# 44 zero matmuls of 128 rows in place of 60 of one row, ahead of the first transform of a Fourier and feed-forward kernel

## The chip, the cores and the metric

The kernel runs on one core of a Trainium2 chip. The metric is the device time of one execution in microseconds (us). The kernel before takes 2027.63 us (median of 7 runs, from 2026.54 to 2028.21).

## The reference

The input x holds 8 sequences of 3008 rows by 256 channels. The real part of its two-dimensional Fourier transform goes row by row through a feed-forward layer with the ELU function:

```python
X = np.fft.fft(np.fft.fft(x, axis=1), axis=2)
h = X.real.reshape(B * S, D) @ w_in            # (24064, 256) @ (256, 2048)
g = np.where(h > 0.0, h, np.exp(np.minimum(h, 0.0)) - 1.0)
return g @ w_out                               # (24064, 2048) @ (2048, 256)
```

The weights arrive as 64-bit floats; the kernel sees them as pairs of 32-bit words.

## The kernel before

**The steady part.** The symmetry of a real input lets the kernel do one column of the sequence transform for two output rows. Its 8 x 1504 columns are cut into tiles of 256. A tile takes eight steps, and each step treats two of the 16 blocks of 128 hidden units: TensorE multiplies the cosine half of the transform (ring buffer Rr) by folded weights Wc and the sine half (Ir) by Ws, VectorE, ScalarE and GpSimd form the ELU of the sum and of the difference, and TensorE multiplies the results by the second weights into four accumulators in PSUM (pA to pD).

**The order of work.** All work is put into one list of events with due times (`at`, line 983; a step's period is 4.8), sorted by time, and then emitted. Nearly every compute instruction is pinned, so each engine runs its own instructions in just that order. Events with times below zero are the preamble. This case is about the preamble.

**What the preamble does**, with the names that the profile shows:

- SyncE (SP) issues the loads: the first chunk of w_in (`raw`, line 193), two of the four quarters of x for sequence 0 (`xl`, lines 153 and 154; GpSimd issues the other two as indirect transfers, line 144), the channel matrix `CC` (line 964), the first cosine and sine matrices `MC` (`load_mats`, line 319: MC00, later MC10, and at last MC01 and MC11), and further chunks of the weights.
- A weight chunk is turned from 64-bit words into f32 by `fields` (VectorE, lines 211 and 217), `power` (ScalarE, line 359 by way of `act`), `round` (VectorE line 242, for some chunks GpSimd line 356) and `scale` (VectorE, lines 254 and 260).
- `fold_x` (line 413; instructions on lines 419 and 439) adds and subtracts the quarters of x into the inputs of the transforms: `e` for the cosine, `o` for the sine. `fold_first` (line 464) makes `xb`, the input for one extra channel.
- TensorE's order (every matmul is on line 347): the zero matmuls into bank M; `fold_chunk(0)`, eight matmuls `H<-w,CC` that fold weight chunk 0; `R_even`, six matmuls into pA and six into pB (`<-MC,e`); `x_even`, six into pC and six into pD (`<-MC,xb`); `I_even`, six into pA and six into M (`<-MC,o`); then the first step's matmuls, `fold_chunk(1)` and so on.
- ScalarE's order: `put_chunk(0)` (copies the folded chunk to Ws and Wc), `power` of w_in chunk 1, the copy of pA for `R_even` (`bs`), the copy of pC for `x_even`.
- VectorE's order: the folds of x, `fold_first`, `fields` and `round` of w_in chunk 1, `scale` of it, then `plus` and `minus` (line 353) of `R_even` into Rr, the same of `x_even` into Rb, then `fields` of w_in chunk 2, and so on. The first step's `even_part` (line 708, tile E) also needs `wex`, which SP brings in two hops: `wx<-Ws` (line 385) and `wex<-wx` (line 387). On SP that second hop stands behind `Ir<-Rb` (line 1036), which waits for `x_even`.

**The lines that change.** `zero` is made on line 333 and cleared on line 334. The loop on lines 959 and 960 is the first thing in TensorE's queue:

```python
mm(idle, zero[:, 0:128], zero[:, 0:1].to_broadcast([1, 512]), True)
```

Its weights are one row of 128 zeros, its moving operand is one zero that is read 512 times, and `idle` is PSUM bank M. Nothing reads what these matmuls write; bank M is written anew by `I_even`.

Of the kernel before, what the change touches and what calls it, by code (L numbers as in the profile page):

```python
# [10 lines left out]
BF = mybir.dt.bfloat16  # L11
# [66 lines left out]
def kernel(  # L78
# [17 lines left out]
    cpool = ctx.enter_context(tc.tile_pool(name="consts", bufs=1))  # L96
# [233 lines left out]
    pick = cpool.tile([128, 32], FP, tag="pick")  # L330
    nc.vector.memset(R4, 0.0)
    nc.vector.memset(Rx4, 0.0)
    zero = cpool.tile([1, 264], BF, tag="zero")
    nc.vector.memset(zero, 0.0)
    row_tables()
    r128_dr = dpool.tile([NB, HALF], FP, tag="r128", name="r128")
# [4 lines left out]
    def bank(tag):  # L341
        bufs = 3 if tag == "H" else 1
        return ppool.tile([128, 512], FP, tag=tag, bufs=bufs, name=tag)

    def mm(out_, lhsT, rhs, start, stop=True):
        pin(
            nc.tensor.matmul(  # L347
                out_, lhsT=lhsT, rhs=rhs, start=start, stop=stop, skip_group_check=True
            )
        )  # L350
# [377 lines left out]
    def exp_neg(ap):  # L728
        act(ap, ap, func=AF.Exp, scale=-1.0)
# [226 lines left out]

    state = {}
    idle = bank("M")
    for _ in range(60):
        mm(idle, zero[:, 0:128], zero[:, 0:1].to_broadcast([1, 512]), True)  # L960
    exp_neg(warm)
    w1_chunks[0].load()
    L_first = load_x(0)
# [291 lines left out]
```

## Time and profile before

| what | value |
|---|---|
| median of 7 runs | 2027.63 us |
| the profiled execution, its own time | 2033.98 us |
| its span, first to last instruction | 2031.9 us |
| TensorE busy | 1990.4 us (98%), 8878 matmuls |
| VectorE / ScalarE / GpSimd busy | 1290.1 / 858.4 / 1349.8 us |
| mean granted TensorE clock | 0.994 |
| DMA bytes | 71.60 MB, mean 35 GB/s |

Engines: PE is TensorE's matmul, PEld its weight load, DVE VectorE, ACT ScalarE, POOL GpSimd, SP SyncE; a q behind a name is the engine's queue, which also issues transfers. In `out<-in`, `128*128` is rows by columns of the weights and `128x256` the moving operand. A matmul's recorded duration holds the time through the array too, so the rate of a stream of matmuls is read from the distance between starts, or from the pieces of the chain of waits, which don't overlap. The chain of waits follows the work that ended last back to what released each piece. The clock column (PEclk) is 1.00 where the record shows no throttle.

### The profile page before, as it was taken

How to read it: one execution, taken by the hardware profiler on the slowest of the kernel's cores; microseconds unless marked ns; L12 is line 12 of the kernel's file. 1: busy time of each engine (PE TensorE's matmuls, PEld its weight loads, DVE VectorE, ACT ScalarE, POOL GpSimd, SP SyncE). 2: the span in 40 equal slices, each digit the busy share in tenths (PEclk: the TensorE clock that was granted, in tenths of full speed). 3: DMA queues.
4: the chain of work that ended last, by engine and by line, in shares of the span. 5: the costliest groups of instructions: out<-in, count | busy, mean ns of one | idle time of the engine just before them, and what ended most of it. 6: DMA issues, size and time to landing. Idle time of an engine off the chain costs nothing.

```text
span 2031.9 us, 26762 instructions
## 1 busy us (share of the span) xinstructions
PE 1990.4 (98%) x8878; PEld 1659.3 (82%) x8878; DVE 1290.1 (63%) x2353; ACT 858.4 (42%) x1646; POOL 1349.8 (66%) x1843
## 2 busy tenths in 40 slices
PE   8889899999999999999999999999999999999997
PEld 4678688888888888888888888888888888888886
DVE  6976456666566666666566665666656665566665
ACT  1444334444344443444344444444434444344443
POOL 1688666777477764877657775677757776455564
PEclk9999999999999999999999999999999999999999
DMA  7218410120001210121111111002110010100101
GB/s 304 81 28 8 93 20 11 29 76 16 11 14 27 73 20 14 17 50 42 25 16 19 42 43 28 11 19 73 19 21 11 19 22 14 16 11 13 19 11 21
DMA packets 256253, 71.60 MB, mean 35 GB/s; under 512 B 244512, under 2 KB 245302, under 8 KB 255604
## 3 DMA queue, kind: packets, MB, share of 16 engines
q1 hardware_dynamic: 253780, 57.32, 15.1%
q0 software_dynamic: 2336, 12.59, 1.9%
q8 instruction: 70, 1.15, 0.2%
q14 instruction: 67, 0.55, 0.1%
HBM read 45.02 MB, written 24.80 MB: 34 GB/s over the span
## 4 chain that ended last, share of the span: by engine, by line
PE 90%; DVE 3%; SPq 2%; DMA 2%; POOL 2%; issue 1%; ACT 0%; DVEq 0%; POOLq 0%; ACTq 0%
PE H L347 36%; PE pC L347 16%; PE pB L347 15%; PE pD L347 15%; PE pA L347 7%; POOL G L356 1%; PE M L347 1%; SPq L558 1%; DMA x<-in_x_dram 1%; DVE E L708 1%; SPq L893 0%; DVE G L734 0%; DVE pow L211 0%; DVE w L260 0%; DVE pow L254 0%
## 5 line engine op out<-in xcount | busy, mean ns | idle before, releaser
L356 POOL TENSOR_TENSOR G<-G 128x256 f32<-128x256 f32 x1504 | 1083.2, 731 | 607.1 <-DVE G L734 436.2
L708 DVE SCALAR_TENSOR_TENSOR E<-Rb,wex,H 128x256 f32<-128x256 f32 x752 | 328.0, 477 | 651.3 <-PE H L347 651.1
L359 ACT ACTIVATE G<-H 128x512 f32<-128x512 f32 x376 | 224.5, 597 | 975.9 <-DVE G L718 975.9
L347 PE MATMUL H<-Ir,Ws 128*128 128x256 f32 x1504 | 388.4, 381 | 10.4 <-DVE E L708 10.3
L347 PE MATMUL pC<-G,WT 128*128 128x256 f32 x1504 | 390.3, 382 | 2.3 <-DVE u L353 2.3
L347 PE MATMUL H<-Rr,Wc 128*128 128x256 f32 x1504 | 386.4, 379 | 0.0
L347 PEld LDWEIGHTS H<-Rr,Wc 128*128 128x128 f32 x1504 | 285.1, 190 | 53.2 <-issue 2.5
L347 PEld LDWEIGHTS H<-Ir,Ws 128*128 128x128 f32 x1504 | 279.8, 190 | 58.5 <-DVE E L708 13.2
L347 PEld LDWEIGHTS pC<-G,WT 128*128 128x128 f32 x1504 | 282.6, 190 | 54.2 <-issue 14.0
L718 DVE SCALAR_TENSOR_TENSOR G<-E,H 128x512 f32<-128x512 f32 x376 | 256.0, 681 | 26.5 <-POOL G L356 2.0
L734 DVE SCALAR_TENSOR_TENSOR G<-G,H 128x512 f32<-128x512 f32 x376 | 253.6, 675 | 27.8 <-ACT G L359 27.8
L734 DVE SCALAR_TENSOR_TENSOR G<-M,G 128x512 f32<-128x512 f32 x376 | 256.7, 683 | 0.0
L347 PE MATMUL pB<-G,WT 128*128 128x256 f32 x752 | 229.9, 387 | 5.4 <-POOL G L356 5.3
L359 ACT ACTIVATE G<-G 128x512 f32<-128x512 f32 x376 | 233.4, 621 | 0.0
L347 PE MATMUL pA<-G,w 128*128 128x256 f32 x752 | 224.5, 380 | 4.1 <-DVE Ir L353 4.0
L359 ACT ACTIVATE M<-G 128x512 f32<-128x512 f32 x376 | 224.4, 597 | 0.0
L347 PE MATMUL pB<-G,w 128*128 128x256 f32 x752 | 224.1, 380 | 0.0
L347 PE MATMUL pD<-G,WT 128*128 128x256 f32 x752 | 223.9, 379 | 0.0
L347 PE MATMUL pD<-G,w 128*128 128x256 f32 x752 | 223.7, 379 | 0.0
L359 ACT ACTIVATE M<-M 128x512 f32<-128x512 f32 x376 | 221.1, 588 | 0.1
L347 PEld LDWEIGHTS pB<-G,WT 128*128 128x128 f32 x752 | 138.5, 190 | 40.0 <-POOL G L356 23.3
L347 PEld LDWEIGHTS pA<-G,w 128*128 128x128 f32 x752 | 142.8, 190 | 24.4 <-issue 4.4
(131 smaller groups left out, 1363.8 us busy)
## 6 DMA issues: line engine op xcount, KB each, us to landing
out_dram<-ot SPq DMA_DIRECT2D x504, 32.0 KB
xl<-in_x_dram SPq DMA_DIRECT2D x16, 768.0 KB
MC<-dft_mats SPq DMA_DIRECT2D x4, 1131.0 KB
out_dram<-ot SPq DMA_DIRECT2D x256, 2.0 KB
Rb<-r SPq DMA_DIRECT2D x10, 376.0 KB
raw<-in_moe_w_in_dram SPq DMA_DIRECT2D x6, 512.0 KB
raw<-in_moe_w_out_dram SPq DMA_DIRECT2D x6, 512.0 KB
out_dram<-ot SPq DMA_DIRECT2D x64, 28.0 KB
```

The costliest lines, as they stand in the source:

```text
L347: nc.tensor.matmul(out_, lhsT=lhsT, rhs=rhs, start=start, stop=stop, skip_group_check=True)
L356: pin(nc.gpsimd.tensor_tensor(out=o, in0=a, in1=b, op=op))
L359: pin(nc.scalar.activation(out=o, in_=i, func=func, **kw))
L558: nc.sync.dma_start(out=t[:, s0:s1], in_=bass.AP(tensor=xt, offset=x.offset + row * ND + 128, ap=[[SEQ * ND, NB], [step * ND, s1 - s0], [1 ...
L708: nc.vector.scalar_tensor_tensor(out=S.E[:, c], in0=Rb[:, cols(i)], scalar=wex[:, f : f + 1], in1=S.H[:, c], op0=ALU.mult, op1=ALU.add,)
L718: nc.vector.scalar_tensor_tensor(out=two(S.G[:, 0:512])[:, :, ::-1], in0=two(S.E), scalar=2.0, in1=two(S.H), op0=ALU.mult, op1=ALU.subtract,)
L734: nc.vector.scalar_tensor_tensor(out=o, in0=e, scalar=-1.0, in1=h, op0=ALU.add, op1=ALU.max)
```

## The change

The tile of zeros becomes 128 rows by 128 columns. The loop issues 44 matmuls instead of 60, and each uses all 128 rows of the array; the moving operand is a zero column of 128 rows, read 512 times. Nothing else differs.

```diff
-    zero = cpool.tile([1, 264], BF, tag="zero")
+    zero = cpool.tile([128, 128], BF, tag="zero")
     nc.vector.memset(zero, 0.0)
...
     idle = bank("M")
-    for _ in range(60):
-        mm(idle, zero[:, 0:128], zero[:, 0:1].to_broadcast([1, 512]), True)
+    for _ in range(44):
+        mm(idle, zero, zero[:, 0:1].to_broadcast([128, 512]), True)
```

## The prediction

> **What bounds the kernel now.** The page first: PE is busy 98% of the span, and the chain of work that ended last is 90% PE. From 120 us on, all that PE waits for comes to 12.6 us (6.0 for POOL's xe, 3.7 and 2.3 and 0.6 for three others), so from there a PE-bound stream follows whose work the change leaves alone. What the change touches lies ahead of 120 us, so I read the chain of waits for the first 60 us; the columns are start, length, engine, tile, line.
>
> ```profile
> 1.20 25.78 PE M L347 x60
> 26.98 3.55 PE H L347 x8
> 30.52 1.90 PE pA L347 x6
> 32.43 1.90 PE pB L347 x6
> 34.33 1.91 PE pC L347 x6
> 36.23 1.92 PE pD L347 x6
> ...
> 38.25 1.00 DVE Rb L353 x2
> ```
>
> The 60 zero matmuls stand on the chain with all their 25.78 us. The first useful matmuls follow them without a gap, and VectorE's Rb at 38.25 waits for the last of these. So the zeros delay the start; how far they can shrink depends on what else is late.
>
> **The rate of a zero matmul.** The rows of the tile zero, then TensorE's timeline:
>
> ```profile
> L347 PE MATMUL M<-zero x60: 602/629/629, 1.2 to 26.3; 1*128 1x512 bf16 x60
> ```
>
> ```profile
> 26.91 3.62 PE L347 MATMUL H<-w,CC 128*128 128x256 f32 x8
> ...
> 56.35 1.89 PE L347 MATMUL H<-w,CC 128*128 128x256 f32 x8
> ```
>
> Zeros start (26.35 - 1.20)/59 = 0.426 us apart. The same eight matmuls H<-w,CC take 3.45 us from their first start to the next tile's at 26.91, and 1.73 at 56.35: 0.431 against 0.216 each. Right behind the zeros TensorE ran at half rate, and at 30.5 the transform pA runs at 0.317 for 377 columns, full rate. So 25 us of unbroken one-row matmuls did not open the clock, and 3.45 us of full-row matmuls did. The clock column reads 1.00 here; durations decide, since its first recorded change is the later one:
>
> ```profile
> 47.00:48.00 1.00, 0.00 (x0) 0.00 (x0) 1.00 (x4) 0.91 (x2) 0.00 (x0) 0.65 0.95 358
> 54.00:55.00 1.00, 1.00 (x4) 0.57 (x3) 0.90 (x2) 0.00 (x0) 0.00 (x0) 0.94 0.63 219
> ```
>
> In the clock column, the third from the end, a mean of 0.65 and of 0.94 puts the drop to half at 47.30 and the rise at 54.1. Finer stretches give drops at 71.2 and 91.7, rises at 74.6 and 95.1. The distances, 6.8, 17.1, 3.4, 17.1 and 3.4 us, are multiples of 3.4: the clock seems to be decided on a grid of 3.41 us. Full-row work from 49.15 needed 4.95 us to open it, from 71.63 2.95; a drop came after 2.6 to 3.6 us without a matmul.
>
> **The change, term by term.**
>
> *Removed:* 16 matmuls. At 0.426 that is 6.8 us on the chain.
>
> *Changed:* the other 44 use all rows. The trace has no full-row zeros. One bound is that they run like the one-row zeros: 44 x 0.426 = 18.8, ending near 20.1. The other is that they open the clock as H<-w,CC did. Half rate then lasts between 2.95 us and, if the start falls just behind a grid point, 6.8 (two windows). In D us at half rate D/0.426 matmuls run, and the rest take 0.213 each (0.426 x 0.216/0.431): 44 x 0.213 + D/2 = 10.9 to 12.8, ending at 12.1 to 14.0. I take this one: the nearest rows, full-row work on this engine, opened the clock each time, and what differs is only the values.
>
> The Trainium skill ("TensorE: Matmul & The Clock Gate", Part 1) says that some 3.4 us of sustained matmul activity open the gate, with no word of rows. The 25.78 us row speaks against that. By the rule alone the old zeros would have run fast from about 5 us on, and only 16 x 0.213 = 3.4 us would go.
>
> *The memset* of zero (0.17 us) becomes wider and shorter; R of 128x32 f32 took 0.09. At most 0.1 us, on the chain; taken as nothing.
>
> **What is late next.** With the zeros over by 14.0, fold_chunk(0) runs at full rate (1.73) until 13.9 to 15.8; its weight chunk left DVE by 8.9. Then the transforms need e, and DVE's timeline gives the rest:
>
> ```profile
> 16.20 1.95 DVE L419 TENSOR_TENSOR e<-e,e 128x768 f32<-128x768 f32 x2
> ...
> 24.65 0.69 DVE L242 SCALAR_TENSOR_TENSOR w<-raw,w 128x512 f32<-128x512 uint32 x1
> 31.86 0.69 DVE L254 SCALAR_TENSOR_TENSOR pow<-raw,pow 128x512 int32<-128x512 int32 x1 [6.51 <-ACT pow L359]
> 32.59 0.69 DVE L260 SCALAR_TENSOR_TENSOR w<-w,pow 128x512 f32<-128x512 f32 x1
> 34.44 0.55 DVE L353 TENSOR_TENSOR Rr<-bs,pB 128x377 f32<-128x377 f32 x1 [1.16 <-PE pB L347]
> ...
> 38.25 0.55 DVE L353 TENSOR_TENSOR Rb<-bs,pD 128x377 f32<-128x377 f32 x1 [2.74 <-PE pD L347]
> ```
>
> The reader is to see the brackets: idle time before an instruction and who ended it. DVE sat idle 6.51 + 1.16 + 2.74 = 10.4 us, each time because PE was late (the 6.51 through ACT, whose power of chunk 1 stands behind put_chunk, and that waited 16.2 us for PE H). Without PE's lateness DVE runs on: L242 ends at 25.34, L254 and L260 end by 26.8, R_even's plus, minus and one column take 1.07 (34.44 to 35.51), so Rb could start at 27.8.
>
> Does PE make that? e is ready at 18.15. pA to pD take 7.6 at full rate, ending at 25.8. But PE idles from 13.9-15.8 to 18.15, so the clock may close; half rate for up to 4.95 us (the row of 49.15) costs 2.5, and pD ends at 28.3. So Rb starts between 27.8 and 28.4 instead of 38.25: **9.9 to 10.4 us earlier**. I take 10.3, as DVE's own queue hides most of a closed clock. Here the same page of the Trainium skill speaks against the change: it warns that a PE gap over about 3 us returns the gate to half rate. The row of 47.3 agrees; the rule would charge the transforms some 1.7 us (half of 3.4), nearly all under DVE.
>
> *Matrices:* MC00 was issued at 2.70. SP's waits tell when loads landed:
>
> ```profile
> SPq L193 <- DMA raw<-in_moe_w_in_dram: 0.2, 1, 0.2
> ```
>
> ```profile
> SPq L319 <- DMA MC<-dft_mats: 0.8, 1, 0.8
> ```
>
> The first ended at 16.9: a w_in chunk issued behind MC00 had landed. The second ended at 22.3, for MC10, which I_even needs only after 25.8. Both match loads landing in the order of issue.
>
> *wex:* the one transfer that loses its cover. DMA is full until 35.0 (share 0.93 to 1.0, then 0.09). wx<-Ws would be issued near 23.5 instead of 30.97, and wex<-wx near 30.3 at the earliest. It took 3.9 us (40.64 to 44.55). If wx is not held up, wex lands by 34.2; if both wait for the queue to drain, at 35 + 1.1 (wx's own wait at 52.67) + 3.9 = 40.0. The first E, at 48.31 now, is due at 38.0. So 0 to 2.0 us; I take 0.3, as a 1 KB read behind one 512 KB load should be quicker than with three behind it.
>
> *Behind Rb* the chain goes DVE, ACT, POOL, DVE on chunk 2, whose data landed by 19; it moves as a whole. Chunk loads of line 193 at 40 to 42 move with it and are used at 80 us and later. PE's 6.0 us for xe hangs on loads issued at a step, so it moves too.
>
> **Sum:** 10.3 - 0.3 = 10.0 us off the profiled span of 2031.9 (2033.98 for the execution). That execution is 6.35 above the median; I take the same difference off the median: 2027.6 - 10.0 = **2017.6**, own range 2017.0 to 2019.8.
>
> **The rivals.**
>
> *Zeros don't open the clock* (the change then does only half of what it says): all-zero data in full rows counts as little as one row. For it: no row shows zeros opening the clock. Against: 60 one-row matmuls differ from the openers in rows as well. Saving 16 x 0.426 = 6.8: fold_chunk(0) at 20.2 and at half rate as before. **2020.8.**
>
> *Something downstream takes part back:* wex at its late bound, with raw loads and the grid's phase against it, 3 to 5 us lost: **2021.6** (own range 2020.6 to 2023.5). The chain shows only 2.0 of it.
>
> *A transform matrix lands late* (slower): PE never waited for MC00 because it asked only at 30.4. If it landed then, PE would idle until 30.4, start at half rate, and pD would end at 30.4 + 7.6 + 2.5 = 40.5, against 38.15: 2.3 us slower, **2029.9**. It decides from a landing after 28.1. The SP wait that ended at 16.9 speaks against it.
>
> **How the numbers follow.** The clock opens and DVE sets the start: 0.72. Zeros don't open it: 0.15. Part given back: 0.08. Late matrix, or anything near no change: 0.04. Slower for it by more: 0.01. The range from 2016.5 to 2021.3 holds the first two and half of the third. This kernel's measurement tells 0.2%, 4.1 us, from no change: faster 0.95, same 0.04, slower 0.01.
>
> **What would show it.** The 44 zeros should change from 0.43 to 0.21 us apart at 4 to 8 us and end at 12 to 14; pA should start near 18.2; DVE should run without an idle stretch until Rb near 28; the first E should come near 38, and every later PE piece 10 us earlier. I am wrong if zeros stay 0.43 apart, if pA starts well after 18.2, or if E waits for wex long after 38.

## The result, and the profile after

The changed kernel takes 2017.01 us (median of 16 runs), the kernel before 2027.21 (38 runs): 10.2 us less, ratio 0.9952, 95% interval 0.9943 to 0.9961 (the ratio is estimated from all runs; that of the medians is 0.9950). The forecast was 2017.6, from 10.0 us less; 2017.01 lies at the fast edge of its own range, 2017.0 to 2019.8.

TensorE's timeline of the changed kernel; columns as before, with the idle time ahead of an instruction and who ended it in brackets:

```profile
1.14 11.87 PE L347 MATMUL M<-zero 128*128 128x512 bf16 x44 [1.14 <-DVE zero L334]
12.86 1.89 PE L347 MATMUL H<-w,CC 128*128 128x256 f32 x8
18.30 3.32 PE L347 MATMUL pA<-MC,e 128*128 128x377 f32 x6 [3.56 <-DVE e L419]
21.41 2.65 PE L347 MATMUL pB<-MC,e 128*128 128x377 f32 x6
23.90 2.06 PE L347 MATMUL pC<-MC,xb 128*128 128x377 f32 x6
25.80 2.06 PE L347 MATMUL pD<-MC,xb 128*128 128x377 f32 x6
...
39.63 2.07 PE L347 MATMUL H<-Ir,Ws 128*128 128x256 f32 x4 [5.37 <-DVE E L708]
41.50 2.84 PE L347 MATMUL pB<-MC,e 128*128 128x376 f32 x6
44.18 2.06 PE L347 MATMUL pC<-MC,e 128*128 128x376 f32 x6
```

The 44 zeros take 11.7 us from their first start to the next tile's, where 44 at the old distance of 0.426 would take 18.7. The eight matmuls behind them last 1.89 us, as the same form did at 56.35 in the kernel before; right behind the one-row zeros they took 3.62. Then PE waits 3.56 us for e. The bracket is the new limit in its first form: PE asks for the transform's input and VectorE hasn't made it.

VectorE's timeline of the same kernel:

```profile
24.74 0.69 DVE L242 SCALAR_TENSOR_TENSOR w<-raw,w 128x512 f32<-128x512 uint32 x1
25.35 0.68 DVE L254 SCALAR_TENSOR_TENSOR pow<-raw,pow 128x512 int32<-128x512 int32 x1
26.07 0.69 DVE L260 SCALAR_TENSOR_TENSOR w<-w,pow 128x512 f32<-128x512 f32 x1
26.68 0.54 DVE L353 TENSOR_TENSOR Rr<-bs,pB 128x377 f32<-128x377 f32 x1
...
27.98 0.55 DVE L353 TENSOR_TENSOR Rb<-bs,pD 128x377 f32<-128x377 f32 x1 [0.24 <-PE pD L347]
...
38.71 0.87 DVE L708 SCALAR_TENSOR_TENSOR E<-Rb,wex,H 128x256 f32<-128x256 f32 x2 [0.68 <-DMA wex<-wx]
```

Of the three idle times of before (6.51, 1.16 and 2.74 us) only 0.24 is left, and Rb starts at 27.98 instead of 38.25. One new bracket has come: the first E waits 0.68 us for wex. The chain of waits of the first 60 us therefore no longer runs through TensorE but through this transfer:

```profile
14.96 8.85 DMA w<-in_moe_w_out_dram
...
23.87 11.64 DMA wx<-Ws
35.53 3.07 DMA wex<-wx
```

wx<-Ws, 1 KB, is issued at 23.87 behind the big loads and lands at 35.5, when these are nearly through (385 to 434 GB/s from 23 to 35 us, 362 in the next us, 174 in the one after).

**The two profiled executions differ by more than the medians** (spans of 2031.9 and 2017.7, 14.2 us apart). At 129 us of the old one and 119 of the new one the matmuls H<-MC,xd stand 10.2 us apart; that is the change. On the way there the lead isn't steady. It is 10.27 us at Rb and only 9.52 at the first E and at the matmuls behind it, since wex was late. The old kernel's next lines, to be read against those at 39.63 to 44.18 above, give it back:

```profile
49.15 2.08 PE L347 MATMUL H<-Ir,Ws 128*128 128x256 f32 x4 [4.61 <-DVE E L708]
51.01 3.61 PE L347 MATMUL pB<-MC,e 128*128 128x376 f32 x6
54.46 2.06 PE L347 MATMUL pC<-MC,e 128*128 128x376 f32 x6
```

From H<-Ir,Ws to pC the old kernel took 5.31 us and the new one 4.55, because the clock opened 4.95 us after the first of these matmuls in the old one and 3.4 us after it in the new one. At pC the lead is 10.28 again; in the next 50 us it moves between 8.98 and 11.83 before it settles at 10.2.

The rest of the 14.2 us lies where PE waits for the extra channel, the old kernel's line first:

```profile
PE H L347 <- POOL xe L356: 6.0, 1, 6.0
```

```profile
PE H L347 <- POOL xe L356: 3.0, 1, 3.0
```

With the wait of 6.0 us the clock closed meanwhile, so the 24 matmuls on xe took 3.5 us instead of 2.2: in all 4.3 us. The change isn't seen to have a hand in it: eight of the profiled executions below (e2 to e6, e9 to e11), with late starts as in the old kernel (e5, e6) and with early ones, have no such wait and need 1894.7 to 1896.0 us from H<-MC,xd to the end of the span, where the change's needed 1898.9 and the old kernel's 1902.9.

### The profile page after: what moved, and what is told of

Same layout as the page of the kernel before. It is cut to its first block, busy times and chain, and to the rows that moved or that the text cites. A ratio compares the mean times of both kernels' runs of the same rounds, so it can differ in the third digit from the quotient of the medians.

```text
span 2017.7 us, 26730 instructions
## 1 busy us (share of the span) xinstructions
PE 1974.4 (98%) x8862; PEld 1653.9 (82%) x8862; DVE 1289.3 (64%) x2353; ACT 858.4 (43%) x1646; POOL 1349.3 (67%) x1843
## 4 chain that ended last, share of the span: by engine, by line
PE 92%; DVE 3%; DMA 2%; POOL 2%; issue 1%; SPq 0%; ACT 0%; DVEq 0%; POOLq 0%; ACTq 0%
PE H L347 37%; PE pC L347 16%; PE pB L347 16%; PE pD L347 15%; PE pA L347 8%; POOL G L356 1%; DMA wx<-Ws 1%; DMA xl<-in_x_dram,ix 1%; DVE E L708 0%; DMA w<-in_moe_w_out_dram 0%; DVE G L734 0%; DVE pow L254 0%; DVE w L260 0%; DMA out_dram<-ot 0%; DMA xl<-in_x_dram 0%
## 5 line engine op out<-in xcount | busy, mean ns | idle before, releaser
L734 DVE SCALAR_TENSOR_TENSOR G<-G,H 128x512 f32<-128x512 f32 x376 | 253.6, 675 | 27.8 <-ACT G L359 27.8
```

What stands on the lines that cost most here:

```text
L734: nc.vector.scalar_tensor_tensor(out=o, in0=e, scalar=-1.0, in1=h, op0=ALU.add, op1=ALU.max)
```

## The experiments

The theory: full rows open the clock, which empties PE's front; from there VectorE's queue, and at last wex, set the start. The rivals: the smaller count alone did it; or an open clock at the first transforms is worth something by itself.

**Rows alone (e1).**

```diff
-    for _ in range(44):
+    for _ in range(60):
```

> 60 zero matmuls, now of 128 rows: the rows alone. Theory (full rows open the clock, then VectorE's queue and the wex transfer set the start): zeros 0.43 us apart up to some 5 us and 0.21 after, over at 12.9 + 16 x 0.213 = 16.3; the folding of chunk 0 ends at 18.0, so hardly a gap before the transform pA at 18.3, which starts at full rate; Rb at 27.7; the first E still waits for wex at 38.7. About 2017.0 us, as the change. Rival 1 (only the smaller count gave the gain): about 2027. Rival 2 (the clock at the first transforms is what counts, so an open clock there gives more): some 2 us less than the change, 2015.

Measured: 2017.45 us, ratio to before 0.9962 (0.9952 to 0.9972). TensorE's timeline, then VectorE's:

```profile
15.93 1.89 PE L347 MATMUL H<-w,CC 128*128 128x256 f32 x8
18.29 2.17 PE L347 MATMUL pA<-MC,e 128*128 128x377 f32 x6 [0.46 <-DVE e L419]
```

```profile
27.65 0.54 DVE L353 TENSOR_TENSOR Rb<-bs,pD 128x377 f32<-128x377 f32 x1
...
38.80 0.87 DVE L708 SCALAR_TENSOR_TENSOR E<-Rb,wex,H 128x256 f32<-128x256 f32 x2 [1.12 <-DMA wex<-wx]
```

The 16 zeros that the change took away cost nothing once the rows are full: they fill PE's wait for e. The transforms now run at full rate, 1.7 us of PE time is saved, and Rb comes 0.33 earlier, E not at all: the wait for wex grows from 0.68 to 1.12. In the five profiled runs with full-row zeros and both hops of wex on SyncE's queue (the change, e1, e7, e8, e11) E starts at 38.56 to 38.80, wherever Rb lies between 27.41 and 27.98. Both rivals fall. Behind E this execution loses 1.2 us to the change's (H<-MC,xd at 119.99 against 118.77), since the clock opened only 5.9 us after the first matmul behind E, and not 3.4: where the clock's grid falls moves a single execution by about as much as the medians of the change, e1 and e3 differ.

**Count alone (e2).**

```diff
-    for _ in range(60):
+    for _ in range(44):
         mm(idle, zero[:, 0:128], zero[:, 0:1].to_broadcast([1, 512]), True)
```

> 44 zero matmuls of one row: the count alone. Theory: zeros stay 0.426 us apart and end near 20.0; the folding of chunk 0 follows at half rate; Rb near 31.4 instead of 38.25; 6.8 us off the kernel before, about 2020.4. Rival 1 (only the count matters): as the change, 2017.0. Rival 2 (only the rows matter): as before, 2027.

Measured: 2019.81 us, ratio 0.9965 (0.9952 to 0.9978), 7.0 us under the 2026.82 of the kernel before beside it. TensorE's timeline:

```profile
1.20 18.95 PE L347 MATMUL M<-zero 1*128 1x512 bf16 x44 [1.20 <-DVE zero L334]
20.08 3.38 PE L347 MATMUL H<-w,CC 128*128 128x256 f32 x8
23.30 2.06 PE L347 MATMUL pA<-MC,e 128*128 128x377 f32 x6
```

The zeros stay 0.43 us apart and chunk 0 runs at half rate, as before, only 6.83 us (16 x 0.427) earlier. VectorE's Rb follows, forecast near 31.4, still behind PE:

```profile
31.18 0.55 DVE L353 TENSOR_TENSOR Rb<-bs,pD 128x377 f32<-128x377 f32 x1 [2.74 <-PE pD L347]
```

VectorE's idle time on account of PE is 3.4 us here (0.70 and 2.74), of 10.4 before; 0.24 is left in the change and nothing in e1. So the count alone brings 7.0 us, the rows alone 9.4 and both 10.2 (the last two aren't apart by their intervals): they don't add up, since either one pushes PE's front towards the same wall.

**No zeros (e3).**

```diff
-    idle = bank("M")
-    for _ in range(44):
-        mm(idle, zero, zero[:, 0:1].to_broadcast([128, 512]), True)
```

> No zero matmuls at all. Theory (VectorE's queue hides a closed clock): the folding of chunk 0 starts when its inputs are there, between 9 and 15 us, at half rate; the transforms start near 18.3 at half rate for 3 to 5 us; pD ends by 28.4 and Rb starts by 28.5; E waits for wex at 38.7 as in the change: 2017.0, at most 0.5 more. Rival (the warm-up is needed): the transforms run at half rate all through, pD ends at 33.5, and the time is 2022 or more.

Measured: 2016.37 us, ratio 0.9949 (0.9936 to 0.9962). TensorE, then VectorE:

```profile
12.66 3.75 PE L347 MATMUL H<-w,CC 128*128 128x256 f32 x8 [12.66 <-DMA CC<-chan_mats]
18.17 3.83 PE L347 MATMUL pA<-MC,e 128*128 128x377 f32 x6 [1.76 <-DVE e L419]
```

```profile
27.82 0.55 DVE L353 TENSOR_TENSOR Rb<-bs,pD 128x377 f32<-128x377 f32 x1 [0.21 <-PE pD L347]
...
38.32 0.87 DVE L708 SCALAR_TENSOR_TENSOR E<-Rb,wex,H 128x256 f32<-128x256 f32 x2 [0.46 <-DMA wex<-wx]
```

Chunk 0 and pA run at half rate, and still Rb starts where it did. Chunk 0 waits for CC until 12.66, and the change's zeros were over at 12.86, so they held PE up by no more than 0.2 us. The warm-up as a whole is worth nothing that these medians can tell; the kernel before paid 10 us for it.

**wex on a queue of its own (e4 and e9).** In `spread_last_row`, for the first piece only, both hops go to GpSimd's queue (e4) or ScalarE's (e9):

```diff
-        nc.sync.dma_start(out=wx_dr[:, c], in_=Ws[127:128, c])
+        eng = nc.scalar if q == 0 else nc.sync
+        eng.dma_start(out=wx_dr[:, c], in_=Ws[127:128, c])
         with nc.allow_non_contiguous_dma(reason="one row to columns"):
-            nc.sync.dma_start(
+            eng.dma_start(
...
```

> The change, with the two hops of the first wex (wx<-Ws, wex<-wx) issued from GpSimd's queue instead of SyncE's, where the big loads stand ahead of them. Theory: wex lands well before 38, the first E starts at 38.0 instead of 38.7, and the time is 0.7 us less than the change: 2016.3. Rival (the wait for wex was covered by something else): 2017.0. Should the transfers on this queue wait for the same busy engines, wex lands no earlier, and it is 2017.0 too, with the wait still in the trace.

> The change, with the two hops of the first wex issued from ScalarE's queue. GpSimd's queue took the wait for wex away (the first E followed VectorE's own work) at a median of 2015.8, but its profiled execution also had x landing 1.1 us late. Theory: a queue without the big loads is all that counts, so E starts at 38.0 with no wait for wex, and the time is 0.7 us under the change, 2016.3. Rival: the late x was caused by the move to GpSimd's queue; here x lands as before (first fold of xl at 6.5) and the gain is larger, 2015.5 or less. If this queue's transfers also land only when the loads drain, E waits for wex as in the change, 2017.0.

Measured: 2015.77 (e4; ratio 0.9946, 0.9934 to 0.9959) and 2016.22 (e9; 0.9955, 0.9941 to 0.9968). ScalarE's timeline of e9, then VectorE's:

```profile
15.96 0.48 ACTq L386 DMA_DIRECT2D wx<-Ws  x1
20.56 0.47 ACTq L388 DMA_DIRECT2D wex<-wx  x1
```

```profile
27.26 0.54 DVE L353 TENSOR_TENSOR Rb<-bs,pD 128x377 f32<-128x377 f32 x1
...
37.21 0.86 DVE L709 SCALAR_TENSOR_TENSOR E<-Rb,wex,H 128x256 f32<-128x256 f32 x2
```

The second hop goes out 4.6 us after the first instead of 11.7, and the bracket in front of E is gone. E follows Rb by 9.95 us, as in the kernel before (9.98), where the change has 10.73: that is the 0.7 us. The other 0.7 by which E comes early is Rb's own (27.26 against 27.98), with x at hand 0.4 us sooner and a clock that stayed open. What the queue does isn't separated from what an earlier issue does: on ScalarE's queue the first hop also goes out at 15.96 instead of 23.87, with fewer loads ahead of it.

In e4 the wait for wex is gone too, but E comes later than in the change:

```profile
39.09 0.86 DVE L709 SCALAR_TENSOR_TENSOR E<-Rb,wex,H 128x256 f32<-128x256 f32 x2
```

There x landed late, so the first fold of xl started at 7.7 us (6.6 in the change, 6.2 in e9). e10 and e12 below have a late x as well (7.3), on ScalarE's queue. So three of the four profiled executions with the hops moved have it, and none of the ten others (6.2 to 6.6): the move may cause it, which these runs don't settle. The gain of 0.7 us is thus seen in one trace, e9's; in the medians it has about the right size, but the intervals overlap that of the change.

**No zeros, wex on ScalarE's queue (e10)**, both diffs together.

> No zero matmuls, and the first wex from ScalarE's queue. Theory: the two are independent; no zeros costs nothing and wex gives 0.7 us: 2015.7 (2016.4 measured without zeros, less 0.7). Rival (the zeros matter once wex is out of the way, because then PE's half rate sets Rb): pD would end later than 27.8 and Rb with it; 2016.4 or more.

Measured: 2015.42 us, ratio 0.9942 (0.9928 to 0.9955), the lowest median of all, though not apart from the change by its interval. VectorE's timeline:

```profile
29.97 0.55 DVE L353 TENSOR_TENSOR Rb<-bs,pD 128x377 f32<-128x377 f32 x1 [1.48 <-PE pD L347]
```

In this execution x landed 1.1 us late, which moves both engines, and half rate lasted through pA and part of pB, some 6.1 us of matmuls (pA and pB took 6.85 us, 3.81 at full rate) where e3 had 3.5. So PE did set Rb, by 1.48 us. The profiled execution of e12 below, with the same front, shows the same (1.55). The rival is thus right in two executions, not in the median: without zeros the cover is thin.

**How many rows (e5, e6, e11) and columns (e7).** 60 zeros each:

```diff
-    for _ in range(44):
-        mm(idle, zero, zero[:, 0:1].to_broadcast([128, 512]), True)
+    for _ in range(60):
+        mm(idle, zero[0:64, 0:128], zero[0:64, 0:1].to_broadcast([64, 512]), True)
```

and in the same way 32 and 96 rows; for e7, 128 rows with `zero[0:128, 0:32]` as weights, written to `idle[0:32]`.

> 60 zero matmuls of 64 rows. If the clock opens for a stream of matmuls of half the rows, the zeros are 0.21 us apart after some 5 us, are over near 16.3, and the first E comes near 38.7 (span near 2015 to 2018, as the change). If half the rows are too few, they stay 0.43 apart to the end, over near 26.9, and the matmuls of chunk 0 behind them run at half rate (span some 10 us longer). The theory only says that 128 rows open it and one row doesn't; this row says on which side 64 lie.

> 60 zero matmuls of 32 rows: the same reading as with 64. If the rows that carry work are what counts, 32 may stay closed where 64 open; zeros then end near 26.9 with the span some 10 us longer. If only a single row was too few, they end near 16.3.

> 60 zero matmuls of 96 rows. 64 rows left the clock at half rate, 128 rows opened it, with 128 or 32 columns. If the share of rows has to pass some bound between 64 and 96, the zeros are over near 16.3 to 17 and the span is near 2015 to 2021; if the bound lies above 96, they stay 0.43 us apart, end near 26.9, and the span is near 2024 to 2025.

> 60 zero matmuls of 128 rows and only 32 columns of weights. If rows alone count, the clock opens near 5 us and the zeros are over near 16.3. If the share of the whole array in use counts, this is a quarter of it, as 32 rows of 128 columns are, and the two should go the same way: over near 26.9 if a quarter is too little.

The line of the tile zero in each, 64 rows first, then 32, 96, and 128 rows by 32 columns. The numbers after the count are ns (shortest, median, longest), then the first and last start in us:

```profile
L347 PE MATMUL M<-zero x60: 606/631/632, 1.1 to 26.3; 64*128 64x512 bf16 x60
```

```profile
L347 PE MATMUL M<-zero x60: 601/626/626, 1.1 to 26.3; 32*128 32x512 bf16 x60
```

```profile
L347 PE MATMUL M<-zero x60: 378/379/634, 1.1 to 16.4; 96*128 96x512 bf16 x60
```

```profile
L347 PE MATMUL M<-zero x60: 377/379/634, 1.1 to 16.3; 128*32 128x512 bf16 x60
```

32 and 64 rows never open the clock in 25 us; 96 do, and so do 128 rows with a quarter of the columns. A quarter of the array by rows and a quarter by columns go opposite ways: rows count, and for these matmuls the bound lies between 64 and 96. One execution each: 2027.00 and 2026.02 us for the closed ones, 2017.11 for 96 rows. The 2023.06 of e7 holds a wait of 5.4 us for xe with the clock closing there, so it says nothing on the zeros; its H<-MC,xd starts at 118.97, as in the change (118.77).

**The extra channel one step later (e8, e12).** fold_ext, dft_ext, ext_side, ext_rows and the first spread_ext that reads them move by one step:

```diff
-    at(25 * T + 1.35, fold_ext)
-    at(25 * T + 4.75, dft_ext)
+    at(26 * T + 1.35, fold_ext)
+    at(26 * T + 4.75, dft_ext)
...
```

> The change, with the fold, the transform and the rows of the extra channel (line 585 and what follows it) each put one step later, so that PE asks for xe some 5 us later. Two profiled executions differ there: PE waited 6.0 us for xe and its clock closed, in the other 3.0 and it stayed open. Theory: this wait is a matter of how fast a long row of small transfers runs, it is what the two profiled spans differ by beyond 10 us, and it is what makes some executions some 8 us longer than the rest; one step later PE doesn't wait there, the long ones disappear (all within 2 us), and the median is 0 to 3 us less than the change, 2014 to 2017. Rival: the wait moves with the consumer and the long executions stay as they are, 2017 with some at 2023 to 2026.

> No zero matmuls, the first wex from ScalarE's queue, and the extra channel's consumers one step later. Theory: as without the last edit, 2015.7, and no execution more than 2.5 us above the median, since PE no longer meets a late xe. One step later cost the change some 0.7 us of median against its other version, so 2016.4 is the upper end. Rival (the late executions come from elsewhere): some lie 6 us or more above the median here too.

Measured: 2017.71 us (e8, from 2016.86 to 2018.96; ratio 0.9956, 0.9942 to 0.9970) and 2016.79 (e12, from 2015.53 to 2019.25; 0.9947, 0.9934 to 0.9961). Neither median is where it was forecast (2014 to 2017, and 2015.7). The wait for xe is gone from both traces, and no execution is over 2.5 us above its median, while of the change's runs and e9's some lie 6 to 8.5 us above. That would fit the theory of the long executions, but it doesn't show it. The traces of e2, e3, e4, e9, e10 and e11 have no wait for xe either, and the runs of e2, e3 and e10 no long execution, all without this edit. And ten are too few: 3 of the 16 runs of the change were long, and at that rate ten in a row without one happen 13 times in 100. The median did not fall, so a typical execution doesn't wait there. As a version to keep it brings nothing that these runs can tell.

## Why the prediction was right

- *Zeros at full rate.* Forecast: half rate for 2.95 to 6.8 us, the zeros over at 12.1 to 14.0. Measured: over at 12.9; with 0.216 per fast one and 0.426 for a slow one, 11.7 us means some 10 slow ones, 4.5 us. The clock's grid agrees: four steps of 3.41 us ahead of the drop at 19.17 lie at 5.5, which is 4.4 us behind the first start.
- *Gap and clock.* pA was forecast near 18.2, with a clock that may have closed. It started at 18.30 and pD ended at 27.9, inside 25.8 to 28.3; the clock closed at 19.2 and opened at 22.6 (the clock column is the third from the end):

```profile
19.00:19.50 0.50, 0.50 (x2) 0.20 (x1) 0.50 (x2) 0.00 (x0) 0.00 (x0) 0.67 0.97 406
22.50:23.00 0.50, 0.50 (x3) 0.24 (x2) 0.50 (x1) 0.00 (x0) 0.00 (x0) 0.92 1.02 373
```

The worst case in the forecast was too mild, though: it took one row's 4.95 us of half rate, where the same grid allowed two windows (6.8) for the zeros. e10 and e12 had some 6.1 us, and Rb started 1.5 us behind VectorE's queue. That the change's execution had 3.4 us is where the grid fell.

- *VectorE as the wall.* Rb forecast at 27.8 to 28.4, measured at 27.98: 10.27 us earlier, against 10.3. That a half-rate start of the transforms costs nearly nothing is shown by e1 and e3: e1 runs them all at full rate, e3 the first six at half, and Rb starts at 27.65 and 27.82. It holds for some 3.5 us of half rate, not for the 6.1 of e10.
- *wex.* Forecast 0 to 2.0 us, 0.3 taken; measured 0.68, so this term was undersized by 0.4. That wex held E is shown by E's steady 38.6 to 38.8 and by e9; that both hops went out behind the loads and the first landed with their end is in the trace, while e9 doesn't tell the queue from the earlier issue. The first hop landed at 35.5, near the late bound of 36.1; the second took 3.07 instead of 3.9.
- *The carry.* 10.2 us at 119 us, 10.2 in the medians, against 10.0: part of this is luck. The terms that the prediction priced come to 9.5 us at the first E (10.27 less what the late wex took). The missing 0.8 came back right behind E, because the clock opened 1.55 us sooner after the first matmul there than in the old execution. Nothing in the prediction forecast that, and in e1's execution the same stretch ran the other way.
- *The rivals.* "Zeros don't open the clock" is settled by the trace: they do, values notwithstanding; its price of 6.8 us is what the count alone measures (7.0). The late matrix did not occur: in e3 and e1 pA waits for e, never for MC. What was given back downstream is the 0.68 of wex.
- *What the prediction did not see:* it put the gain down to zeros that are quicker. With the wall at VectorE known, it could have said that the zeros, quick or not there at all, come out alike (2017.0, 2017.5, 2016.4). It gave no time for the landing of CC either, which holds chunk 0 back until 12.66 in e3; it stayed hidden because the zeros ended just behind it.

The Trainium skill ("TensorE: Matmul & The Clock Gate", Part 1) sets the warm-up at some 3.4 us of sustained matmuls. With 96 or 128 rows the traces agree within their grid (4.5 us here, 3.7 to 6.0 in e1, e4, e7, e8, e9 and e11, worked out in the same way); with 1, 32 and 64 rows 25 us did not do it, and there the measurement decides.

## What to carry to other kernels

A warm-up of TensorE is work in its queue: read first what ends the wait of the first real matmul's consumer, and count how much idle time of the *next* engine is PE's doing, since that sum (10.4 us here) is all that any shortening can give. Read the rate of a warm-up from the distance between starts, not from the clock column, and give it full rows (96 of 128 were enough here, 64 were not), or leave it out where another engine's queue covers a half-rate start. When PE's front moves up, look for small transfers that now go out behind big loads on the same queue.

## What the runs showed of the hardware

- The clock column shows 1.00 until the first recorded change, though the matmuls of the old kernel's first 30 us ran at half rate (0.431 against 0.216 us for the same eight).
- The clock opens by rows in use, in these back-to-back bf16 matmuls of 512 columns: 25 us with 1, 32 or 64 rows did not open it, 3.7 to 6.0 us with 96 or 128 rows did. 32 columns of 128 are enough (e7), and zeros open it as data do.
- Its closing and opening lie on a grid: in the changed kernel 19.17, 22.58, 39.65, 43.03, 60.13 and 66.96 us, 3.4, 17.1, 3.4, 17.1 and 6.8 apart. Where the grid falls differs between executions: the same matmuls from 39.6 and 39.7 us needed 3.4 us to open it in the change and 5.9 in e1.
- A 1 KB transfer issued at 23.87 us behind big loads on its queue took 11.6 us. Issued on ScalarE's queue at 15.96 (e9) it took at most 4.6, with the DMA engines just as full (share 1.0); how much of that is the queue and how much the earlier issue, these runs don't tell.
